# 34 instead of 20 filler products ahead of the first transposes of an attention and gated-FFN kernel

## The chip, the cores and the metric

The kernel runs on one core of one Trainium2 chip. The core has TensorE (PE, matrix products; its weight loads are listed apart as PEld), VectorE (DVE), ScalarE (ACT), GpSimd (POOL) and SyncE (SP). Each has its own queue of instructions and runs it in order; they wait for each other through semaphores. Data come from main memory by DMA. The metric is the device time of one execution in microseconds (us), the median of several runs.

## What is computed

An attention layer over 4 batches, 8 heads, 768 positions and 64 features per head, and behind it a gated feed-forward layer over the 3072 resulting rows of 512 features. Three heads are full causal, five see only a window of 64 positions and 4 sink positions.

```python
scores = scale * np.matmul(q, k.transpose(0, 1, 3, 2))
scores = np.where(mask[None, :, :, :], scores, -1000000000.0)
a = np.exp(scores - max); a = a / (np.sum(a, axis=-1, keepdims=True) + 1e-09)
x = np.matmul(a, v)        # then to rows of 512 features
g = x @ w_gate;  gelu = 0.5 * g * (1.0 + erf(g * inv_sqrt2))
ffn_out = gelu * (x @ w_val) @ w_out
out = x + (1.0 / (1.0 + np.exp(-(x @ w_res)))) * ffn_out
```

## The kernel before

The 24 tiles of 128 positions are worked in six chunks of four (`CHUNKS`). For a chunk the kernel brings q and k into feature-major form, forms the scores of each pair of heads on TensorE, takes the exponential on ScalarE, multiplies by a mask on VectorE, multiplies by v on TensorE, normalizes, transposes the result, and then runs the gated layer over it: gate and value products (with the tiles `wg`, `wv`), their product `hT`, the output product (`wo`) and the residual gate (`wr`). Work of neighbouring chunks is interleaved.

Every operation is a `Task` of a graph, with its engine and what it depends on. The order is written out by hand: `PLAN` is a list of task numbers, and `schedule` walks it from left to right, puts each task at the end of its engine's queue, and takes the buffers that `PLACES` names. A word of the form w20 in the plan stands for 20 fillers:

```python
        for x in "".join(PLAN).split():
            if x[0] == "w":
                for _ in range(int(x[1:])):
                    t = next(fillers)
                    t.bufs[0].fixed = t.bufs[0].pool.quiet("warm")
                    if t.bufs[0].fixed is not None:
                        place(t, "pe")
```

A filler (line 1468) multiplies a 128x128 block of zeros (`blank`) with a 128x256 block of zeros into a PSUM bank that nothing else holds at that place; nobody reads it. It depends only on the memset of `blank` (line 511). 180 are made, 33 are placed, all in the first 17 us.

The start of the program is the part that matters here. Four DMAs (line 656, two on SP's and two on ACT's queue) bring the first two tiles of k and q. Eight casts (lines 662 and 663, task name c16, on DVE and ACT) turn them to 16 bit. Four groups of eight transposes (line 670) turn q and k of the two tiles, each group into its own PSUM bank, from where DVE or ACT copies it to `qT` or `kT` (line 680). Two more tiles come by POOL's DMAs (line 542) into `qks` and are transposed at line 726 and copied at line 737. Scores are line 895, those against the sink positions line 986; the exponentials are lines 911, 915 and 993 and write `es`, `ea`, `eb`, `ek`. Products with v are lines 477 and 1019. Line 477 is also the helper of the gate, value, residual and output products, and line 478 its form by halves of the columns.

On TensorE's queue the first block of fillers stands first, then the four groups of transposes at line 670, five fillers, two groups of scores, two groups of transposes at line 726, more scores, three fillers, and so on. On DVE's queue the order there is: cast of q, two memsets of `vk` (line 535), cast of q, copy of `ident` (line 514), cast of k, copy of the first `qT`, cast of q's second tile, copies of `kT` and `qT`. The third and fourth groups of transposes follow the first two in order; the fourth needs that last cast. The scores need the last copy of `qT`.

Of the kernel before, what the change touches and what calls it, by code (L numbers as in the profile page):

```python
# [48 lines left out]


PLAN = (
    "0 17 18 214 217 211 1 220 199 212a 216 6 7 15 218a 16 2 215 8 w20 225 219a 4 3 213 223 226 9 10 222 5 227 221a 228 229 "
    "230 11 12 232 224a w5 420 421 423 425 247 248 231 251 233 234 424 417 418 252 419 236 w3 431 433 432 245 235 246a 427 "
    "249 254 428 429 w2 467 434 468 250 472 435 436 473 422 241 200 437 201 464 465 203 239 240 426 237 238 202 242 w3 440 "
    "441 442 430 481 483 438 439 449 443 482 444 455 450 451 457 466 456 452 453 458 454 459 475 478 479 469 470 204 484 "
# [1511 lines left out]
```

## Time and profile before

| | before |
|---|---|
| median of 3 runs | 260.44 us (260.28 to 261.14) |
| profiled execution | 261.0 us |
| its span, first to last instruction | 259.3 us |
| TensorE busy | 250.1 us |
| VectorE, ScalarE, GpSimd busy | 203.0, 164.9, 105.1 us |
| TensorE idle ahead of the first transposes | 2.27 us |

The profile gives for every instruction its start from the beginning of the span, its length, its engine and its line. A row of the timeline merges neighbouring instructions of one kind; the bracket at its end is the idle time of the engine before it, and what ended it. A row for a group gives least, median and most length in ns. A product's length holds its way through the array, so that products in a row overlap; their spacing is what a block costs. [...] The chain of waits follows the last instruction back through what released it.

### The profile page before, as it was taken

To read this page: it belongs to the slowest core of one execution; us is meant where nothing else is said; L and a number is where in the kernel's file an instruction comes from. 1 tells how busy PE (TensorE), PEld (TensorE's weight loads), DVE (VectorE), ACT (ScalarE), POOL (GpSimd) and SP (SyncE) were. 2 spreads that over 40 slices of the span, in tenths; PEclk is the share of its full clock that TensorE was granted. 3 is DMA by queue.
4 is the path that set the end of the run, shared out by engine and by line. 5 is a ranking of instruction groups with operands and counts; after the bars stand their busy time and mean duration, and the time that the engine had idled before them with its cause. 6 is when DMAs were issued, how large, how long until landed. Compare 5 with 4: busy or idle time off the path is not lost.

```text
span 259.3 us, 8020 instructions
## 1 busy us (share of the span) xinstructions
PE 250.1 (96%) x3393; PEld 176.1 (68%) x3393; DVE 203.0 (78%) x453; ACT 164.9 (64%) x298; POOL 105.1 (41%) x144
## 2 busy tenths in 40 slices
PE   6798999999999999999999999999999999999992
PEld 4567644558577677667678567689578678678891
DVE  2599424899989998587998587999777887768975
ACT  2489862996566995565887365894456997265410
POOL 8992920765960829268604077003310010120031
PEclk9999999999999999999999999999999999999999
DMA  8999999995999999999979999506998005360003
GB/s 152 168 201 207 193 199 203 155 147 76 164 157 220 207 129 110 175 234 141 167 73 132 243 128 162 38 8 73 134 154 261 5 4 83 38 89 4 3 20 142
DMA packets 104115, 33.69 MB, mean 130 GB/s; under 512 B 90768, under 2 KB 99216, under 8 KB 104080
## 3 DMA queue, kind: packets, MB, share of 16 engines
q0 software_dynamic: 72592, 18.36, 79.5%
q1 hardware_dynamic: 29120, 13.91, 28.9%
q10 hardware_dynamic: 2368, 0.92, 1.5%
q8 instruction: 26, 0.43, 0.7%
q14 instruction: 9, 0.07, 0.1%
HBM read 29.36 MB, written 10.49 MB: 154 GB/s over the span
## 4 chain that ended last, share of the span: by engine, by line
PE 93%; DVE 2%; DMA 2%; ACT 1%; issue 1%; DVEq 0%
PE ps L477 49%; PE ps L478 31%; PE ps L895 6%; DMA qks<-in_q_dram 2%; PE ps L1019 2%; PE ps L726 1%; PE ps L1115 1%; PE ps L1468 1%; PE ps L986 1%; PE ps L670 1%; DVE otile L1409 1%; DVE x L663 0%; DVE vk L535 0%; ACT vs L622 0%; ACT es L911 0%
## 5 line engine op out<-in xcount | busy, mean ns | idle before, releaser
L1413 POOL DMA_DIRECT2D out_dram<-otile x16 | 15.4, 995 | 84.9 <-DVE otile L1409 54.7
L542 POOL DMA_DIRECT2D qks<-in_q_dram x35 | 32.5, 950 | 17.5 <-issue 8.6
L477 PE MATMUL ps<-xT,wg 128*128 128x512 f16 (+1 forms) x172 | 38.4, 337 | 0.0
L542 POOL DMA_DIRECT2D qks<-in_k_dram x35 | 32.8, 973 | 12.8 <-PE ps L726 12.8
L477 PE MATMUL ps<-xT,wv 128*128 128x512 f16 (+1 forms) x166 | 37.9, 338 | 0.0
L1183 ACT ACTIVATE gact<-ps 128x512 f16<-128x512 f32 x38 | 22.1, 595 | 23.8 <-PE ps L477 16.3
L1185 DVE SCALAR_TENSOR_TENSOR hT<-gact,ps 128x512 f16<-128x512 f16 x38 | 25.8, 685 | 10.8 <-ACT gact L1183 5.3
L1257 DVE TENSOR_TENSOR ps<-ps,otile 128x256 f32<-128x256 f32 x60 | 24.9, 431 | 9.8 <-PE ps L478 5.1
L542 POOL DMA_DIRECT2D va<-in_v_dram x24 | 24.1, 1035 | 5.1 <-PE ps L477 5.1
L477 PEld LDWEIGHTS ps<-xT,wg 128*128 128x128 f16 x172 | 16.4, 98 | 11.0 <-ACT gact L1183 0.3
L1353 ACT ACTIVATE srs<-ps 128x512 f32<-128x512 f32 x22 | 13.1, 596 | 15.3 <-PE ps L478 11.6
L477 PEld LDWEIGHTS ps<-xT,wv 128*128 128x128 f16 x166 | 15.9, 98 | 9.9 <-ACT xT L1125 0.3
L911 ACT ACTIVATE ea<-ps 128x1024 f16<-128x1024 f32 (+2 forms) x24 | 21.1, 927 | 0.5 <-PE ps L895 0.5
L1275 ACT ACTIVATE gact<-ps 128x512 f16<-128x512 f32 x30 | 16.9, 598 | 6.7 <-PE ps L478 4.1
L1282 DVE SCALAR_TENSOR_TENSOR hT<-gact,ps 128x512 f16<-128x512 f16 x30 | 19.6, 681 | 1.7 <-PE ps L477 1.7
L1253 ACT ACTIVATE ps<-ps 128x256 f32<-128x256 f32 x25 | 9.2, 370 | 16.9 <-PE ps L477 12.2
L478 PE MATMUL ps<-xT,wv 128*64 128x512 f16 (+1 forms) x156 | 19.2, 341 | 0.0
L1086 DVE TENSOR_TENSOR xtok<-ps,rcp 128x512 f32<-128x512 f32 (+1 forms) x28 | 17.1, 610 | 1.0 <-ACT x L1094 0.4
L477 PE MATMUL ps<-wo,hT 128*128 128x256 f16 (+1 forms) x114 | 17.7, 296 | 0.0
L895 PE MATMUL ps<-qT,kT 64*128 64x64 f16 (+3 forms) x391 | 16.9, 216 | 0.6 <-ACT xT L1125 0.6
L478 PE MATMUL ps<-xT,wg 128*64 128x512 f16 (+1 forms) x144 | 17.3, 344 | 0.0
L1385 DVE TENSOR_TENSOR otile<-otile,ps 128x256 f32<-128x256 f32 x33 | 13.7, 417 | 4.5 <-PE ps L478 3.5
(188 smaller groups left out, 586.6 us busy)
## 6 DMA issues: line engine op xcount, KB each, us to landing
out_dram<-xtok SPq DMA_DIRECT2D x4, 1024.0 KB, 5.5
out_dram<-otile POOLq DMA_DIRECT2D x16, 256.0 KB, 5.0
va<-in_v_dram POOLq DMA_DIRECT2D x24, 128.0 KB, 6.7
qks<-in_q_dram POOLq DMA_DIRECT2D x32, 64.0 KB, 6.4
qks<-in_k_dram POOLq DMA_DIRECT2D x32, 64.0 KB, 6.2
wg<-in_moe_w_gate_dram POOLq DMA_DIRECT2D x3, 512.0 KB, 12.5
wv<-in_moe_w_val_dram POOLq DMA_DIRECT2D x3, 512.0 KB, 12.1
wo<-in_moe_w_out_dram POOLq DMA_DIRECT2D x4, 384.0 KB, 16.5
```

What stands on the lines that cost most here:

```text
L477: return e.matmul(o, lhsT=lhsT, rhs=rhs, **k)
L478: return [e.matmul(o[h:h + 64], lhsT=lhsT[:, h:h + 64], rhs=rhs, **k) for h in (0, 64)][-1]
L542: return G.add(eng, issue, lambda e: e.dma_start(out_ap(), in_ap), list(deps) + (consts if eng == "pool" else []), prio, bufs=bufs, dma=co ...
L895: return [e.matmul(at(scr)[:, oo:oo + w], lhsT=side(BB, qb, low, 1)[half, k0:k0 + 128], rhs=side(BB, qb, low, 0)[half, qq:qq + w], start=T ...
L911: return e.activation(out=o, in_=i_, func=AF.Exp, scale=SM_SCALE)
L1086: t2 = G.add("dve", c_dve(2 * n * 64), lambda e: e.tensor_tensor(out=xview(), in0=avv(0, DHEAD), in1=scale(), op=ALU.mult), [t1] + xdeps, ...
L1183: ta = G.add("act", c_act(512), (lambda gb=gb, ga=ga, gw=gw: lambda e: e.activation(out=at(ga)[:, :], in_=at(gb)[:, gw], func=AF.Gelu))(), ...
L1185: th = G.add("dve", c_dve(512), (lambda vb=vb, ga=ga, f=f, vw=vw: lambda e: e.scalar_tensor_tensor(out=hv(f), in0=at(ga)[:, :], scalar=0.5 ...
L1257: return G.add("dve", c_dve(256), lambda e: e.tensor_tensor(out=at(ps)[:, o], in0=at(ps)[:, BL], in1=at(es)[:, 0:256], op=ALU.add), deps, ...
L1275: ta = G.add("act", c_act(512), (lambda x=x, ga=ga, both=both: lambda e: e.activation(out=two(at(ga)[:, :]), in_=both(x), func=AF.Gelu))() ...
L1282: th = G.add("dve", c_dve(512), (lambda x=x, f=f, ga=ga, both=both: lambda e: e.scalar_tensor_tensor(out=two(hv(f)), in0=two(at(ga)[:, :]) ...
L1413: t = G.add("pool", 1.0, (lambda ot=ot, r0=r0: lambda e: e.dma_start(out[r0:r0 + 128, :], at(ot)[:, :], accum_op=ALU.add))(), ends + [stor ...
```

## The change

One word of the plan changes: the first block has 34 fillers instead of 20.

```diff
 PLAN = (
-    "0 17 18 214 217 211 1 220 199 212a 216 6 7 15 218a 16 2 215 8 w20 225 219a 4 3 213 223 226 9 10 222 5 227 221a 228 229 "
+    "0 17 18 214 217 211 1 220 199 212a 216 6 7 15 218a 16 2 215 8 w34 225 219a 4 3 213 223 226 9 10 222 5 227 221a 228 229 "
```

The numbers 225, 223, 227 and 229 are the four groups of transposes. On TensorE's queue, at the very start of the program, the difference is this (L395 is the jump into the engine's program, `ident,x` the operands of the transposes of the first tiles):

```order
 L395 UNCONDITIONAL_BRANCH
-L1468 MATMUL ps<-blank 128x256 x20
+L1468 MATMUL ps<-blank 128x256 x34
 L670 MATMUL ps<-ident,x 64x128 x32
 L1468 MATMUL ps<-blank 128x256 x5
```

Fourteen fillers more stand ahead of the transposes; nothing else moves on this queue, and the queues of the other four engines are the same. With what each of them waits for, the start of TensorE's queue in the changed program is:

```order
L1468 MATMUL ps<-blank 128x256 [waits cnt_dve]
L1468 MATMUL ps<-blank 128x256 x33
L670 MATMUL ps<-ident,x 64x128 [waits cnt_dve,cnt_pool]
L670 MATMUL ps<-ident,x 64x128 x7
L670 MATMUL ps<-ident,x 64x128 [waits cnt_dve,cnt_act]
L670 MATMUL ps<-ident,x 64x128 x7
L670 MATMUL ps<-ident,x 64x128 [waits cnt_act]
L670 MATMUL ps<-ident,x 64x128 x7
L670 MATMUL ps<-ident,x 64x128 [waits cnt_dve,cnt_act]
L670 MATMUL ps<-ident,x 64x128 x7
L1468 MATMUL ps<-blank 128x256 x5
L895 MATMUL ps<-qT,kT 128x64 [waits cnt_dve,cnt_act]
```

Only the first filler waits (for the memset of `blank`); each group of transposes waits for its casts, and the scores wait for the copies. No wait is added or taken away.

## The prediction

> **What bounds the kernel now.** I read the page first, then the busy time by stages, the chain of waits of the first 24 us, and the timeline of each engine there. First the page's rows on TensorE and the summary of the chain:
>
> ```profile
> PE 250.1 (96%) x3393; PEld 176.1 (68%) x3393; DVE 203.0 (78%) x453; ACT 164.9 (64%) x298; POOL 105.1 (41%) x144
> PEclk9999999999999999999999999999999999999999
> PE 93%; DVE 2%; DMA 2%; ACT 1%; issue 1%; DVEq 0%
> ```
>
> TensorE is busy nearly everywhere and carries 93% of the chain. The view by stages shows where it is the bound without a gap and where it is not (columns: stretch and length, then busy us and instructions of PE, PEld, DVE, ACT and POOL, then granted clock, DMA share, GB/s):
>
> ```profile
> 1.12:5.57 4.45, 4.45 (x20) 2.85 (x20) 0.32 (x4) 1.49 (x2) 3.80 (x10) 1.00 0.89 177
> 9.65:13.88 4.23, 4.23 (x52) 2.77 (x53) 2.07 (x5) 1.55 (x4) 4.06 (x9) 1.00 2.30 160
> 13.59:18.67 5.08, 5.08 (x105) 3.11 (x106) 4.53 (x14) 5.04 (x10) 5.08 (x8) 1.00 1.36 203
> 18.91:21.39 2.48, 1.90 (x30) 1.33 (x22) 2.43 (x10) 2.44 (x5) 0.47 (x1) 1.00 1.24 206
> 21.44:253.00 231.56, 231.53 (x3146) 164.00 (x3148) 186.68 (x409) 152.03 (x273) 85.88 (x109) 1.00 1.10 125
> ```
>
> From 21.44 us on TensorE has work for 231.53 of 231.56 us, so whatever lets that run start earlier is worth its whole length of time at the end. Between 13.59 and 21.39 ScalarE is the full engine (5.04 of 5.08 us and 2.44 of 2.48). Ahead of that stands a chain that is not full anywhere, and there the change sits (start, length, what):
>
> ```profile
> 7.05 0.66 DVE x L663
> 7.71 0.14 issue
> 7.84 1.08 PE ps L670 x16
> ...
> 12.12 0.99 PE ps L726 x16
> ...
> 14.38 0.57 PE ps L726 x16
> ```
>
> The same 16 transposes take 0.99 us at 12.12 and 0.57 us at 14.38. The page's clock row says full speed in all slices, so it does not show this; the durations do. The timeline of TensorE (start, length, operation, count):
>
> ```profile
> 1.12 4.45 PE L1468 MATMUL ps<-blank 128*128 128x256 f16 x20 [1.12 <-DVE blank L511]
> 7.84 1.49 PE L670 MATMUL ps<-ident,x 128*64 128x128 f16 x24 [2.27 <-DVE x L663]
> 9.65 0.64 PE L670 MATMUL ps<-ident,x 128*64 128x128 f16 x8 [0.31 <-ACT kT L680]
> 10.22 1.25 PE L1468 MATMUL ps<-blank 128*128 128x256 f16 x5
> 11.40 0.72 PE L895 MATMUL ps<-qT,kT 64*128 64x64 f16 x15
> 12.05 1.06 PE L726 MATMUL ps<-ident,qks 128*64 128x128 f16 x16
> 13.04 0.50 PE L895 MATMUL ps<-qT,kT 64*128 64x128 f16 x6
> 13.48 0.68 PE L1468 MATMUL ps<-blank 128*128 128x256 f16 x3
> 14.31 0.64 PE L726 MATMUL ps<-ident,qks 128*64 128x128 f16 x16
> 16.74 0.50 PE L1468 MATMUL ps<-blank 128*128 128x256 f16 x3
> L1468 PE MATMUL ps<-blank x33: 272/421/421, 1.1 to 17.0; 128*128 128x256 f16 x33
> ```
>
> A filler costs 421 ns early and 272 ns late (last row, least/median/most). Taking the last one's length off a block, fillers follow each other by (4.45 - 0.42)/19 = 0.212 us in the first block and by (0.50 - 0.27)/2 = 0.115 us at 16.74. The block at 13.48 lies between: 0.68 us against some 0.85 us if all three were slow. So TensorE runs at half speed until about 13.8 us and at full speed after, in this execution. A busy block of 4.45 us (from 1.12) did not bring full speed; one of 4.23 us (from 9.65) did.
>
> **The change part by part.** It adds 14 products of 0.212 us to the first block: 14 x 0.212 = 2.97 us if all are slow. The gap behind the block is 2.27 us (the row at 7.84), and it ends with VectorE's cast, not with TensorE. TensorE would stand busy from 1.12 to the transposes, and on to 9.33: some 8 us, nearly twice either block above. I take it that full speed comes within the fillers. If it comes at time W, the last filler issues at W + (34 - (W - 1.12)/0.212) x 0.115; up to W = 7.0 that is below 7.7, so that the transposes still start at 7.84, when the cast lets them. Each 0.1 us later costs 0.046 us; no full speed at all costs this: the last filler starts at 1.12 + 33 x 0.212 = 8.12, and other work follows a slow filler block by 0.35 us (the block of 10.22 starts its fifth at 11.07, the scores at 11.40), so 8.47 instead of 7.84, **0.63 us late**. I take no delay, with W below 7.0.
>
> Now the work between 7.84 and 13.8 runs at full speed. Transposes come in pairs: seven steps between eight pairs take (1.06 - 0.31)/7 = 0.107 us each at 12.05, (0.64 - 0.24)/7 = 0.057 at 14.31. The lengths are in these rows of line L726, at 12 us and at 14 us:
>
> ```profile
> L726 PE MATMUL ps<-ident,qks x16: 311/313/315, 12.0 to 12.8; 128*64 128x128 f16 x16
> L726 PE MATMUL ps<-ident,qks x16: 219/219/243, 14.3 to 14.7; 128*64 128x128 f16 x16
> ```
>
> A group of eight (four pairs) thus ends 3 x 0.05 + 0.095 = 0.25 us sooner. What waits for it is VectorE, whose rows here stand with those of POOL's DMA issues:
>
> ```profile
> 5.50 0.46 DVE L663 CAST x<-qks 128x256 f16<-128x256 f32 x1 [3.83 <-DMA qks<-in_q_dram]
> 7.75 0.28 DVE L663 CAST x<-qks 128x256 f16<-128x256 f32 x1
> 8.52 0.42 DVE L680 COPY qT<-ps 128x512 f16<-128x512 f16 x1 [0.49 <-PE ps L670]
> 8.86 0.64 DVE L663 CAST x<-qks 128x256 f16<-128x256 f32 x1
> 10.33 0.42 DVE L680 COPY qT<-ps 128x512 f16<-128x512 f16 x1 [0.50 <-PE ps L670]
> 4.92 0.91 POOL L542 DMA_DIRECT2D qks<-in_k_dram  x1
> 7.54 1.85 POOL L542 DMA_DIRECT2D va<-in_v_dram  x2
> 8.50 0.89 POOL L542 DMA_DIRECT2D va<-in_v_dram  x1
> ```
>
> - The copy at 8.52 moves to 8.27, and the cast queued behind it from 8.86 to 8.61. That cast took 0.64 us, ending 0.11 us after the DMA issue of 8.50; the one of 5.50 ended 0.13 us after the issue of 4.92; the one of 7.75, begun 0.21 us into an issue, took 0.28. Moved to 8.61 it begins 0.11 us into the issue of 8.50: nearest the short row. I take 0.28 us, end 8.89 instead of 9.50 (0.61 gained); the other end is 0.64 us again or an end at 9.50, with 0.0 to 0.25 gained.
> - The last eight transposes start 0.14 us behind it, as the first did (the "issue" row at 7.71): 9.04 instead of 9.65, and end 0.61 + 0.25 = 0.86 sooner. The copy at 10.33 moves to 9.47 and ends at 9.89.
> - The scores at 11.40 wait for that copy and stand behind five fillers. The fillers lose 4 x 0.097 + 0.15 = 0.54 us, starting some 0.8 sooner: done at about 10.05, and the copy lets the scores go at 9.89 + 0.14 = 10.03. Scores at 10.05, **1.35 us sooner**.
>
> ScalarE takes it up from there:
>
> ```profile
> 11.84 0.60 ACT L911 ACTIVATE es<-ps 128x512 f16<-128x512 f32 x1 [2.29 <-PE ps L895]
> 12.33 0.76 ACT L915 ACTIVATE eb<-ps 128x256 f16<-128x256 f32 x2
> 13.59 0.81 ACT L911 ACTIVATE ea<-ps 128x768 f16<-128x768 f32 x1 [0.49 <-PE ps L895]
> ```
>
> - The first exponential starts 0.44 us behind the scores' start; their first half is then some 0.1 us faster: 10.05 + 0.33 = 10.38, 1.46 sooner. The three exponentials end 12.33 + 0.76 - 11.84 = 1.25 us later, at 11.63.
> - The next one idled 0.49 us for the scores of 13.04. Those overwrite the bank that the first exponential reads (done at 10.98) and follow the transposes of 12.05, which now run from about 10.45 to 11.0. They start at 11.1 and need about 0.3 us: 11.4, ahead of 11.63. This wait goes; ScalarE is late next, and it is already full. 1.46 + 0.49 = **1.95 us**.
> - ScalarE stays full to 21.39, so its end moves by the same 1.95 and TensorE's long run starts at 19.49 instead of 21.44.
>
> What could stop it is data that arrive by the clock and not by the chain. The tightest is the first piece of the value weights:
>
> ```profile
> 10.97 1.53 POOL L542 DMA_DIRECT2D wv<-in_moe_w_val_dram x2
> 24.96 0.60 PE L477 MATMUL ps<-xT,wv 128*128 128x256 f16 x4
> DMA to landing us min/median/max: 10.3/12.1/16.2
> ```
>
> Issued at 10.97, landed 10.3 us later at 21.3, used at 24.96: moved to 23.0 it still has 1.7 us.
>
> **Sum.** Span 259.3 - 1.95 = 257.4; the profiled execution took 261.0, so 259.05, taken as **259.1**. The median shown is 260.44 (260.28 to 261.14); the profiled execution lies 0.56 above it, near the slowest. I read this scatter as the moment of full speed, which differs between executions, and therefore do not subtract 1.95 from the median.
>
> [...]
>
> **The rivals.**
>
> *The clock stays down, and the fillers are in the way* (slower). The point is a filler block that ends after 7.7; at worst the transposes start at 8.47, and the chain behind them is 0.63 us late: 261.0 + 0.63 = 261.6. For it: 4.45 us of the same products changed nothing. Against it: 4.23 us, with five fillers among them, did. Chance 0.09.
>
> *Some executions of before have full speed early already* (no change). 4.45 us fails and 4.23 us succeeds, so it is not length alone that decides; 20 fillers may be enough in a luckier execution. If the fastest shown, 260.28, was such a one, the change makes every execution like it: 260.3. Against it: by my chain such a run would be 1.95 below 261.0. Chance 0.14. [...]
>
> *Full speed late and the cast held* (little change). With W = 8.0 the last filler issues at 8.2, and the transposes lose about 0.45 us; the cast ends behind the DMA issue, 0.6 more: 259.1 + 1.05 = 260.1. Chance 0.10.
>
> *Transposes stay slow* (little change). Only the five fillers then gain ahead of the scores, 0.5 us; the transposes of 12.05, 1.06 us long, hold the next scores to 12.5 and the exponential to 12.85: 0.75 sooner in all, 260.3. Chance 0.03.
>
> **How the numbers follow.** The forecast, chance 0.64, is 259.1 within 258.5 and 259.7: the upper end is the held cast (0.6), the lower one the same 0.6 for executions whose phase is luckier than the profiled one's. The range reaches up to 260.4 to take in the three cases of little or no change; the slow one is left out. A measurement tells 0.3% from no change, 0.78 us, so faster is below 259.66: nearly all of the forecast, 0.62. Within 0.3%: these three cases and the forecast's upper edge, 0.29. Slower: 0.09.
>
> **What would show it.** In the changed profile: 34 products at L1468 in about 6.6 us, not 7.4, with the later ones 272 ns; first transposes still at 7.84; transposes of 219 ns there; the cast near 8.6 at 0.28 us; the first exponential near 10.4 and no idle time ahead of the one now at 13.59; the gapless run from about 19.5. It is wrong if the transposes start near 8.5, if they still take 314 ns, or if a new gap stands behind 19.5 us.

## The result, and the profile after

| | before | after |
|---|---|---|
| median | 260.33 us (6 runs, 260.05 to 261.14) | 259.14 us (6 runs, 259.08 to 259.20) |
| profiled execution | 261.0 us | 259.19 us |
| its span | 259.3 us | 257.4 us |

The ratio of after to before is 0.9938, with a 95% interval from 0.9917 to 0.9958: 0.6% faster, and the whole interval lies below 1. In these six runs the scatter is 0.12 us, against 1.1 us before; eleven later runs of the changed kernel (last experiment) went from 259.06 to 260.23 us, so part of that is the small number of runs.

TensorE's timeline in the changed kernel (start, length, line, operation, count):

```profile
1.12 6.81 PE L1468 MATMUL ps<-blank 128*128 128x256 f16 x34 [1.12 <-DVE blank L511]
7.86 0.95 PE L670 MATMUL ps<-ident,x 128*64 128x128 f16 x24
9.09 0.41 PE L670 MATMUL ps<-ident,x 128*64 128x128 f16 x8 [0.27 <-DVE x L663]
9.43 0.72 PE L1468 MATMUL ps<-blank 128*128 128x256 f16 x5
10.11 0.46 PE L895 MATMUL ps<-qT,kT 64*128 64x64 f16 x15
10.50 0.64 PE L726 MATMUL ps<-ident,qks 128*64 128x128 f16 x16
```

The 34 products take 6.81 us, not the 7.4 us that 34 would take at half speed: (6.81 - 0.27)/33 = 0.198 us each on average, so the last few ran at full speed. The transposes start at 7.86 (7.84 before): the longer block is not in their way. They run at full speed from the first one on: 24 in 0.95 us, against 1.49. VectorE and GpSimd behind them:

```profile
8.32 0.42 DVE L680 COPY qT<-ps 128x512 f16<-128x512 f16 x1 [0.29 <-PE ps L670]
8.66 0.28 DVE L663 CAST x<-qks 128x256 f16<-128x256 f32 x1
9.54 0.42 DVE L680 COPY qT<-ps 128x512 f16<-128x512 f16 x1 [0.26 <-PE ps L670]
8.50 0.92 POOL L542 DMA_DIRECT2D va<-in_v_dram  x1
```

The fourth cast starts 0.20 us sooner than before and takes 0.28 us instead of 0.64; the last copy is 0.79 us sooner. On ScalarE, whose rows before were at 11.84, 12.33, 13.59 and 18.91 (the last one stands first here):

```profile
18.91 1.08 ACT L911 ACTIVATE es<-ps 128x512 f16<-128x512 f32 x2 [0.24 <-PE ps L895]
```

```profile
10.44 0.60 ACT L911 ACTIVATE es<-ps 128x512 f16<-128x512 f32 x1 [1.22 <-PE ps L895]
10.93 0.76 ACT L915 ACTIVATE eb<-ps 128x256 f16<-128x256 f32 x2
11.57 0.83 ACT L911 ACTIVATE ea<-ps 128x768 f16<-128x768 f32 x1
17.09 1.09 ACT L911 ACTIVATE es<-ps 128x512 f16<-128x512 f32 x2 [0.52 <-PE ps L895]
```

The first exponential is 1.40 us sooner, and the one at 11.57 has no idle time ahead of it, where 0.49 us stood before: 2.02 us sooner. At 17.09 it is 1.82: the wait for scores ahead of it grew from 0.24 to 0.52 us. The view by stages shows the long run of TensorE, from 19.62 instead of 21.44, with 231.45 of 231.48 us busy:

```profile
11.60:16.60 5.00, 4.86 (x97) 2.78 (x95) 4.68 (x14) 4.98 (x11) 4.83 (x10) 1.00 1.79 185
17.10:19.57 2.47, 1.86 (x28) 1.33 (x22) 2.42 (x10) 2.43 (x5) 2.47 (x4) 1.00 1.24 206
19.62:251.10 231.48, 231.45 (x3146) 164.06 (x3148) 186.70 (x409) 152.03 (x273) 86.06 (x110) 1.00 1.12 127
```

The run starts 1.82 us sooner and the span is 1.8 us shorter: nothing is given back in its 231 us. The 0.20 us between 2.02 and 1.82 are lost on VectorE, between 12.4 and 15.2 us: its first mask there is 2.00 us sooner than before (12.43 against 14.43), the one at 15.19 only 1.83 (17.02 before). Rows of before (first three) and of after:

```profile
14.77 0.28 DVE L947 TENSOR_TENSOR eb<-eb,m_causal 128x256 f16<-128x256 f16 x1
16.02 0.28 DVE L622 COPY vs<-va 64x455 f16<-64x455 f16 x1
12.54 1.27 POOL L603 COPY vk<-va 4x130 f16<-4x130 f16 x4
```

```profile
12.78 0.38 DVE L947 TENSOR_TENSOR eb<-eb,m_causal 128x256 f16<-128x256 f16 x1
14.10 0.46 DVE L622 COPY vs<-va 64x455 f16<-64x455 f16 x1
12.57 1.67 POOL L603 COPY vk<-va 4x130 f16<-4x130 f16 x4
```

GpSimd's four copies stay where they were, and one of VectorE's masks and one of its copies, being sooner, now overlap with them: both sides take longer, VectorE by 0.10 and 0.18 us in these two rows. That one causes the other was not tried.

### The profile page after: what moved, and what is told of

Read it like the earlier page. It is cut to its first block, busy times and chain, and to the rows that moved or that the text cites. A ratio compares the mean times of both kernels' runs of the same rounds, so it can differ in the third digit from the quotient of the medians.

```text
span 257.4 us, 8048 instructions
## 1 busy us (share of the span) xinstructions
PE 250.4 (97%) x3407; PEld 176.7 (69%) x3407; DVE 203.1 (79%) x453; ACT 164.7 (64%) x298; POOL 105.5 (41%) x144
## 4 chain that ended last, share of the span: by engine, by line
PE 93%; ACT 3%; DVE 2%; issue 1%; DVEq 0%
PE ps L477 49%; PE ps L478 32%; PE ps L895 5%; PE ps L1468 3%; PE ps L1019 2%; PE ps L1115 1%; PE ps L726 1%; PE ps L986 1%; ACT es L911 1%; ACT ea L911 1%; DVE otile L1409 1%; ACT vs L622 0%; PE ps L670 0%; DVE otile L1385 0%; DVE otile L1419 0%
## 5 line engine op out<-in xcount | busy, mean ns | idle before, releaser
L542 POOL DMA_DIRECT2D qks<-in_q_dram x35 | 33.8, 1010 | 16.6 <-issue 8.3
L542 POOL DMA_DIRECT2D qks<-in_k_dram x35 | 34.4, 1034 | 12.8 <-PE ps L726 12.8
```

The costliest lines, as they stand in the source:

```text
L542: return G.add(eng, issue, lambda e: e.dma_start(out_ap(), in_ap), list(deps) + (consts if eng == "pool" else []), prio, bufs=bufs, dma=co ...
```

## The experiments

The theory: what the fillers bring is full speed, and it is the place of the busy time that counts. The rivals: a length of uninterrupted work (B), the number of products (C), or the mere closing of the gap ahead of the transposes.

### The kernel before, profiled once more

No edit.

> The kernel before, profiled once more, to see whether the moment of full speed differs between executions. [...]

260.24 us, span 258.5. The flip (the first place where fillers follow each other by 0.115 us instead of 0.212) came early this time: 20 fillers in 4.04 us, where they took 4.45. The view by stages (length, busy us of PE, PEld, DVE, ACT, POOL, then the granted clock):

```profile
1.12:4.60 3.48, 3.48 (x17) 2.50 (x18) 0.25 (x3) 1.49 (x2) 2.83 (x9) 1.00 0.76 167
4.65:8.00 3.35, 0.65 (x10) 0.37 (x10) 2.00 (x6) 0.74 (x3) 3.35 (x5) 1.00 1.53 204
8.05:11.40 3.35, 2.94 (x37) 1.97 (x32) 2.16 (x5) 1.25 (x3) 3.35 (x5) 0.50 2.14 167
11.50:14.80 3.30, 3.27 (x78) 2.08 (x78) 2.35 (x5) 3.05 (x8) 3.13 (x8) 1.00 2.06 172
```

The clock column shows 0.50 from 8.05 to 11.40: full speed was granted at 4.6, **taken back at 8.0** and granted again at 11.4, 3.4 us from change to change. The stretch before it was taken back had 0.65 us of work in 3.35: the gap behind the 20 fillers. The phase, as I call the moment of full speed in an execution, differs from the first profile (flip near 13.8), and neither execution has full speed for the transposes of 7.84 and 7.87, but for the first few of the second one, which start ahead of 8.0. (Ahead of the first grant the clock column reads 1.00 although products are slow; it has no record there. In what follows, full speed is said to come where the first clock record of a trace begins, at 13.88 us in the first profile of before; that agrees with the spacing of the products.)

### 24 and 28 fillers

```diff
-w20
+w24    (the other kernel: w28)
```

> 24 fillers, so the first block issues until about 6.3 us: busy 5.2 us, but idle again from 6.5 to 7.84. [...] Rival B (a length of uninterrupted work decides, somewhere between 4.45 and 6 us): flip inside the first block or as soon as it has run that long, and then the gain of 1.2 us of the change.

> 28 fillers, issuing until 7.1 us. [...] Rival B gives 259.1 too, with the flip wherever the needed length ends.

24 fillers: 260.16 us (10 runs, 259.12 to 261.04), ratio 0.9983 [0.9964, 1.0002]: no change that can be told. 28 fillers: 259.26 us (9 runs, 259.12 to 259.80), ratio 0.9947 [0.9929, 0.9965]. In both profiles the flip came inside the block, at 5.8 and 6.5 us. Stages of the profile with 24:

```profile
2.40:5.75 3.35, 3.35 (x17) 2.41 (x16) 0.15 (x1) 1.18 (x2) 2.98 (x8) 1.00 1.23 236
5.80:9.20 3.40, 1.46 (x32) 1.03 (x32) 3.02 (x9) 1.89 (x5) 3.40 (x5) 1.00 1.65 183
9.25:12.60 3.35, 3.35 (x50) 2.21 (x45) 1.21 (x4) 1.25 (x3) 3.31 (x6) 0.50 2.33 158
```

and with 28:

```profile
3.10:6.45 3.35, 3.35 (x18) 2.35 (x17) 0.99 (x2) 0.48 (x2) 3.04 (x5) 1.00 1.33 242
6.50:9.85 3.35, 2.18 (x40) 1.60 (x39) 2.78 (x9) 1.93 (x5) 3.35 (x5) 1.00 1.81 180
9.90:13.25 3.35, 3.35 (x77) 2.07 (x74) 2.55 (x7) 2.81 (x8) 3.27 (x6) 1.00 2.39 156
```

With 24 the speed granted at 5.8 is lost at 9.2, after a stretch with 1.46 us of work in 3.40; with 28 it is granted at 6.5 and kept, after 2.18 in 3.35. So rival B had the flip inside the block, and was wrong about what that is worth: **with 24 it was lost again in the gap**. Nor is there one length of work that brings full speed: the block had run for 3.5 us when it came in the second profile of before, for 4.7 with 24 fillers and 5.3 with 28, for 6.0 in the changed kernel, while 4.45 us in the first profile of before did not bring it. The mere closing of the gap is not needed either: 28 fillers leave 0.92 us of it, and the changed kernel in its second profile 1.22. Among the ten runs with 24 fillers the two that are faster than 260 us, 259.12 and 259.58, have a mean granted clock of 0.997, the others 0.993 or less.

### The same 20 fillers, two microseconds later

```diff
-... 215 8 w20 225 219a 4 3 213 223 226 9 10 222 5 ...
+... 215 8 4 9 10 w20 225 219a 3 213 223 226 222 5 ...
-              [t_blank], 1e9, bufs=[warm], name="warm")
+              [t_blank, consts[7]], 1e9, bufs=[warm], name="warm")
```

The first filler waits for a mask constant of GpSimd; the order on every engine is that of before.

> Only 20 fillers as in the kernel before, but the first one waits for one of GpSimd's mask constants, so that the block runs from about 3.2 to 7.4 us instead of from 1.12 to 5.57. [...] Rival B (length): 4.2 us is shorter than the 4.45 us that did not suffice, no flip within the block, 260 to 261, or a flip some time after 8 us with a part of the gain. Rival C (the 14 more products themselves, not their place, are needed): as B.

259.26 us (10 runs, 259.04 to 259.59), ratio 0.9950 [0.9935, 0.9966]: the gain of the change with no product added. Two rows of its timeline, the stretch ahead of full speed, and the lengths of the fillers (least, median, most, in ns):

```profile
3.13 4.45 PE L1468 MATMUL ps<-blank 128*128 128x256 f16 x20 [3.13 <-POOL m_win L528]
7.76 1.06 PE L670 MATMUL ps<-ident,x 128*64 128x128 f16 x24 [0.19 <-DVE x L663]
4.33:7.74 3.41, 3.24 (x16) 1.91 (x13) 2.17 (x5) 0.55 (x2) 3.41 (x5) 1.00 1.48 202
L1468 PE MATMUL ps<-blank x20: 393/417/417, 3.1 to 7.2; 128*128 128x256 f16 x20
```

All 20 fillers are slow here (median 417 ns, and 4.45 us for the block, as in the first profile of before). Full speed comes at 7.7: just as the transposes start, after a stretch 95% busy (3.24 of 3.41 us). Rival B had it right that there is no flip within the block, but not the time. The block reaches the transposes and leaves 0.19 us of gap: the place of the fillers counts, and 14 products more are not needed. What the place secured here is a busy stretch that ends at the real work, and no empty one behind it.

### 50 fillers

```diff
-w20
+w50
```

> 50 fillers: with the flip near 7.1 us the last 22 follow each other by 0.11 us and the block issues until about 9.5, 1.8 us past the cast. If fillers ahead of the transposes cost what they delay (my rival on fillers in the way, in this kernel for certain): transposes at 9.65 instead of 7.86, all behind them 1.8 us late, 260.9 (260.7 to 261.1). If the chain behind has slack: less, 259.1 to 260.3.

260.39 us (10 runs, 259.92 to 261.18), ratio 0.9996 [0.9981, 1.0012]. The gain is eaten. The number is below what I had expected, because I had taken one phase for all: in the profile the flip was early, the 50 products took 7.22 us, and the transposes started 0.41 us late:

```profile
1.12 7.22 PE L1468 MATMUL ps<-blank 128*128 128x256 f16 x50 [1.12 <-DVE blank L511]
8.27 0.86 PE L670 MATMUL ps<-ident,x 128*64 128x128 f16 x24
```

The run of TensorE then starts at 20.03 instead of 19.62, the same 0.41: the chain has no slack, as the rival on fillers in the way had it. (This execution also stood still for 0.73 us at 216.8; see the last section. That part of its 260.51 us is not the fillers'.)

### The cast and GpSimd's DMA issue

```diff
+    G.tasks[235].deps.append(G.tasks[222])
     G.whole_groups()
```

One wait is added to the kernel before: the DMA issue of 8.50 us now waits for the fourth cast.

> The kernel before with one wait more: GpSimd's DMA issue of 8.50 us waits for VectorE's fourth cast (8.86). If that cast is long because it meets a running issue (my term of 0.28 against 0.64 us), it takes 0.28 us here, and the last transposes start some 0.4 us sooner in relation to the first ones. If it is long for another reason, it takes 0.6 to 0.75 us as in the two profiles of before. The time, 259.9 to 261.1, depends on the clock's phase in this one look and decides nothing.

```profile
8.53 0.42 DVE L680 COPY qT<-ps 128x512 f16<-128x512 f16 x1 [0.49 <-PE ps L670]
8.87 0.28 DVE L663 CAST x<-qks 128x256 f16<-128x256 f32 x1
9.45 0.87 POOL L542 DMA_DIRECT2D va<-in_v_dram  x1 [0.93 <-DVE x L663]
```

0.28 us at the same start as before (8.87 and 8.86), where it took 0.64. So the long cast is one held by a running DMA issue. Not every cast that meets an issue is held: in the twelve profiles of this case, VectorE's casts at line 663 that begin 0.05 to 0.22 us after an issue's start take 0.27 to 0.29 us, and those that begin 0.25 to 0.67 us after it end 0.11 to 0.12 us behind the issue, whatever their start. It is one execution, 261.07 us; it says nothing of the time.

### Two further versions

VectorE's two memsets of `vk` move into its first wait for data. The first version puts the fourth cast ahead of the first copy and keeps 34 fillers; the second puts eight transposes and the copy into the filler block:

```diff
-... 1 220 199 212a 216 6 7 15 218a 16 2 215 8 w34 225 219a 4 3 213 223 226 9 10 222 5 ...
+... 1 15 16 220 199 212a 216 6 7 218a 2 215 8 w34 225 219a 4 3 213 223 222 226 9 10 5 ...
+... 1 15 16 220 199 212a 216 6 7 218a 2 215 8 w26 225 219a 4 3 213 226 w4 223 222 9 10 5 ...
```

> 34 fillers, and on VectorE the two memsets of vk moved into its wait for the first data, and the fourth cast put ahead of the first copy. The cast then needs only its data (7.85): 7.9 to 8.2, or to 8.6 if it meets the issue that ends at 8.51. The last transposes start at 8.75 or sooner instead of 9.09, but the three copies follow each other: last copy 0.1 to 0.35 us sooner, 258.8 to 259.05. If VectorE's copies bound it: no change, 259.1.

> As the one before, but 26 fillers, then the first eight transposes, then 4 fillers, then the rest; the first copy stands ahead of the fourth cast again. First transposes at about 6.9 to 7.0 instead of 7.86, first copy done by 7.9, cast 7.9 to 8.2 or 8.6, last transposes 0.35 to 0.7 us sooner, scores with them (the five fillers between still bind): 258.6 to 258.9. If in some phases the flip comes later, because the transposes count less than fillers: a wider scatter, 258.8 to 260.

The first: 259.15 us (10 runs, 258.79 to 260.62), the second: 258.97 us (10 runs, 258.82 to 260.22). In the profiles the long run starts at 19.32 and 19.34. Chain of waits, one row of each:

```profile
19.32 0.34 PE ps L895 x2
```

```profile
19.34 0.34 PE ps L895 x2
```

The second and the changed kernel were then timed side by side:

> The changed kernel once more, beside the next one on the same chip: 259.1 median, nearly all runs within 259.05 to 259.4, a few up to 260.5 where TensorE stalls late in the program for nothing that the profile shows (0.3 to 0.9 us in two of the profiles so far).

> 26 fillers, eight transposes, 4 fillers, with the memsets out of the way: its long run of TensorE starts at 19.34 us against 19.62 with 34 fillers in the profiles, so 258.85 median, 0.2 to 0.3 us below the changed kernel in this call. If the clock's phase costs it as much in other executions: no difference, 259.1.

34 fillers: 259.16 us (11 runs, 259.06 to 260.23); the split block: 258.97 us (6 runs, 258.81 to 259.12); before: 260.71 us; ratios 0.9944 [0.9926, 0.9963] and 0.9933 [0.9912, 0.9954]. The first of the two had been expected at 258.8 to 259.05 and the split block at 258.6 to 258.9; both came out above that. The intervals overlap, so the versions are not told apart by time; the split version's median was 0.17 to 0.19 us lower both times, less than its 0.28 us sooner start.

## Why the prediction was right, point by point

- **Clock.** I had the flip within the fillers and no delay for the transposes: 7.86. Right. The flip came at 7.1 in the profile, not below 7.0; by the formula as I wrote it W = 7.0 already gives 7.72 for the last filler, not less than 7.7, so the margin was thinner than I said. The last filler started at 7.66.
- **Transposes, copy, cast, scores.** Foreseen 8.27, 8.61 with 0.28 us, 9.04, 10.05; measured 8.32, 8.66 with 0.28, 9.09, 10.11. That the long price is the DMA issue's doing was shown by the run with the added wait (0.28 us at 8.87 instead of 0.64 at 8.86); that a cast 0.16 us into an issue goes free rested on one row, the nearest, and the other profiles bear it out. By what means an issue holds a cast until 0.11 to 0.12 us past its end, and why it does not hold one that begins 0.05 to 0.22 us into it, was not shown.
- **ScalarE.** Foreseen 10.38 and 11.63 with no wait; measured 10.44 and 11.57. The vanished wait of 0.49 us was the larger part of what took the gain from 1.40 to 2.02; the rest is that the three exponentials took 1.13 us to the next one and not 1.25.
- **The long run.** Foreseen 19.49, measured 19.62: I held the gain to be kept while ScalarE is full to 21.39. It is not quite: between my two rows, at 18.67, it waits 0.24 us for scores, and VectorE was nearly as full as ScalarE (4.53 of 5.08 us, then 2.43 of 2.48). In the changed kernel VectorE's rows grew where they overlap with GpSimd's, the chain of waits runs through VectorE to these scores (`xtok`, line 1086, at 15.74), and the wait is 0.52 us. The sum was 0.07 us too small up to 11.57 and lost 0.20 behind it: together the 0.13 us by which it was too large.
- **Sum.** 259.05 foreseen for the profiled execution, 259.19 measured; 259.1 forecast, 259.14 the median; that the median is so near is in part luck, with 0.13 us amiss in the chain. That I did not subtract 1.95 from the median was right: the medians differ by 1.19 us.
- **The rival of early full speed** had a right premise and a wrong end. 20 fillers do bring it in some executions, but such an execution has lost it again at 8.0, and then takes 260.24, not the 259.1 that my chain gave it. No run of before came below 260.04; by this profile that is the reason. It also explains most of the scatter of before: in the 16 runs beside the last two kernels, those with a mean granted clock of 0.991 to 0.993 (in the profile with 0.991, full speed was taken back for 3.4 us) took 260.04 to 260.52 but for one (261.81), those at 1.000 (one late grant in the profile) 260.99 to 261.16. One run at 0.994 (260.91) and three at 0.987 (261.80 to 262.02) fit neither, and no profile was taken of such a one.
- **The moment of full speed** differs between executions, as I read the scatter: near 13.8 in one profile of before and 4.6 us in the other. In the second it changed again at 8.0 and 11.4. The flips of the other kernels came at 5.8, 6.5, 7.1 and 7.7.
- **The rival of slow transposes** is out: they take 219 ns here from 7.9 us on (median of the 32 at line 670), against 314 before.
- **Tightest arrival.** I named the first piece of the value weights, with 1.7 us to spare. It has that. Tighter, and missed, is the copy of `vs` by DMA that the products at line 1019 need near 58 us; in the profile with 28 fillers TensorE waits for it:

```profile
PE ps L895 <- ACT xT L1125: 0.6, 1, 0.6
PE ps L1019 <- DMA vs<-va: 0.2, 1, 0.2
```

So a still sooner start can be lost there. In the two profiles of the split version TensorE does not wait there, and its spans are shorter than those of the changed kernel by 0.2 and 0.3 us; why the medians differ by less stays open.

## What to carry to other kernels

Fillers ahead of the first real products had two things to do here: to bring full speed, which came at 7.7 us behind 3.24 us of work in 3.41 with the later 20; and to come near enough to the first real work, because full speed was lost after 1.46 us of work in 3.40 (24 fillers) and kept after 2.18 in 3.35 (28). It is the place that counts: 20 fillers that end 0.19 us ahead of the transposes did as much as 34 that start 2 us sooner, where 20 at the old place and 24 did not. Their end has to lie ahead of the data in every phase: 50 fillers made the transposes 0.41 us late, and the long run as much. And before a gain at the start is priced from one profile, look at a second: two executions of the same kernel had their slow stretches at different places.

## What the runs showed of the hardware that was not expected

- How busy TensorE was ahead of a change of the clock, over some 3.4 us, the distance from change to change in the second profile of before. Full speed came after 86% (2.93 us of 3.41, the kernel with the added wait), 88% (2.94 of 3.35, the second profile of before, at 11.4), 95% (3.24 of 3.41, the later 20 fillers) and 100% (the first profile of before, 24 and 28 fillers, the changed kernel). It was lost after 43% (1.46 of 3.40, 24 fillers), 25% (0.84 of 3.41, the added wait) and 19% (0.65 of 3.35, the second profile of before). It was kept after 64% in the 3.41 us behind the grant (2.19 us, the second profile of the changed kernel) and 65% (2.18 of 3.35, 28 fillers). Whether this share is what decides, and where a limit lies, was not shown. Rows of the added wait and of the changed kernel's second profile:

```profile
0.64:4.05 3.41, 2.93 (x14) 2.04 (x15) 0.41 (x4) 1.49 (x2) 2.60 (x10) 1.00 0.59 134
```

```profile
4.49:7.90 3.41, 2.19 (x22) 1.74 (x21) 2.20 (x6) 0.75 (x3) 3.41 (x5) 1.00 1.51 202
```

- Full speed was lost with 24 fillers after 1.9 us without work between 5.80 and 9.20; with 28 fillers it was not, after 1.2 us without work between 6.50 and 9.85.
- TensorE stood still once late in the program for nothing that the profile shows, in one of the twelve profiles (the expectation above speaks of two; no second one is in the profiles, and the 0.23 us with 28 fillers end with the copy of `vs`). In the profile with 50 fillers:

```profile
PE ps L478 <- issue: 0.7, 1, 0.7
```

Single runs 1.2 to 1.5 us above their kernel's median (260.62 and 260.22 of the two further versions, with a granted clock of 1.000 and 0.999) may have the same reason; they were not profiled, and the cause stays open. The slowest run of before in the first set, 261.93, has a granted clock of 0.987 and may be another case.
